# A fused sparse attention and gated FFN on one core: PV turned round for the strided heads, exp kept in PSUM, masks of the first batch by TensorE, stores by SyncE

## The chip, the cores and the metric

The kernel runs on one core of a Trainium2 chip. Times are device microseconds; a time is the median of several executions. The profile has its own measure, the span from the first to the last instruction of one profiled execution.

TensorE is the matrix engine (PE in the profile, PEld its weight loads), DVE the vector engine, ACT the scalar engine, POOL GpSimd, SP or SyncE the engine that issues loads. SBUF and PSUM are the two memories in which the program places its tiles; in both kernels every matmul writes a PSUM tile (`ps_...` and `mps` in the views). PV is the product of the masked probabilities with V, U the transposes that turn its result back. A filler is a matmul whose result nobody uses, put where the planner saw TensorE wait in the start. Distances between the starts of matmuls are read from the single records of the trace, which the views shown here merge.

## The reference, cut to what matters

```python
# q, k, v: (8 batches, 8 heads, 576 positions, 64)
scores = q @ k.T / 8
# heads 0-3: causal band of 32;  heads 4-7: causal, key % 32 == query % 32
attn = softmax(where(mask, scores, -1e9)) @ v
x = attn -> (4608 tokens, 512)
out = ((x @ w1) * (x @ w2)) @ w3 @ w_out       # widths 1024, 1024, 512
```

The kernel multiplies `w3 @ w_out` once at its start (W34 below), so that the FFN is two products (a, b), one elementwise product, and one product with W34 (o).

## The kernel before

Heads are handled in pairs; pairs 0 and 1 are local, pairs 2 and 3 strided. Positions are grouped so that a local block has 96 queries and a strided block 72, with at most 128 keys each. Every pair is done in two halves g. A planner inside the program sorts all operations of all engines into fixed orders by a list of costs; so the order of each engine is static, and an engine that waits holds back everything behind it (TensorE for 1.60 us in the hole shown below). Attention of batch b+1 is woven into the FFN of batch b.

The parts that the change touches, shortened:

```python
# scores, keys on partitions: PSUM slot "B" (two of them); then exp to SBUF, then mask in SBUF
matmul(sps[:, h, i*w:(i+1)*w], kT[r_, ks:ks+P], qT[r_, hp, qs:qs+w])
pte = att.tile([P, 2, 288], FP16)
scalar.activation(out=pte, in_=sps, func=Exp, scale=scale)      # ACT; frees the slot
vector.tensor_mul(ptm, pte, mask)                               # DVE, both inputs in SBUF
# PV, old form: weights = ptm (128 columns, zero padded), streamed = [V | 1]  (65 columns)
matmul(xps[:, h, i*65:(i+1)*65], ptms[pslot][0:kr, c0:c0+P], vt[0:kr, ..., :])
# out: queries on partitions; column 64 is the sum.  Normalise, transpose back (U), copy to xT
vector.reciprocal(rcp, xv[..., D]);  vector.tensor_mul(xqs, xv[..., 0:D], rcp)
tensor.transpose(ps_U[:, t*w:(t+1)*w], xqs[...], id16);  copy(xT[hp][:, S*b:S*b+S], ps_U)
# ... FFN tiles a, b, mul, o ...; the stores are issued by ACT
```

The softmax here doesn't subtract the row's maximum and nothing guards it: scores larger than these inputs give would overflow.

## Time and profile before

| | before |
|---|---|
| time, median of 3 runs | 281.95 us (281.72 to 282.17) |
| the profiled execution | 283.71 us, span 282.0 us |
| TensorE busy | 96% |
| first FFN matmul | 42.3 us |
| first FFN matmul to the start of the last matmul | 235.9 us |

Busy times of the engines, granted TensorE clock in 40 slices, and shares of the chain that ended last, from the page of the kernel before:

```profile
PE 270.5 (96%) x2540; PEld 150.5 (53%) x2540; DVE 166.3 (59%) x326; ACT 155.4 (55%) x291; POOL 123.2 (44%) x146
...
PEclk9999999999999999999999999999999999999999
...
PE 83%; DMA 8%; DVE 4%; SPq 1%; ACT 1%; POOL 1%; issue 0%; ACTq 0%; POOLq 0%; DVEq 0%
```

TensorE is nearly always busy (96%), at full clock (mean granted 1.000). The next lines are the engine table over stretches of the span of the kernel before. Its columns are the stretch, its length, then busy time and instruction count of PE, PEld, DVE, ACT and POOL, then clock, DMA share and GB/s.

```profile
30.00:40.00 10.00, 9.95 (x145) 8.62 (x142) 6.21 (x15) 6.04 (x13) 9.58 (x12) 1.00 1.04 339
40.00:50.00 10.00, 9.11 (x108) 5.87 (x107) 6.67 (x14) 6.85 (x15) 8.99 (x10) 1.00 1.09 354
...
120.00:140.00 20.00, 18.39 (x169) 9.65 (x166) 13.64 (x23) 11.32 (x21) 12.70 (x15) 1.00 0.86 267
140.00:160.00 20.00, 20.00 (x213) 11.25 (x213) 13.89 (x26) 12.61 (x24) 10.63 (x13) 1.00 0.65 185
```

From 60 us on TensorE is full in nearly every stretch (19.82 of 20 at 80 to 100), with one hole at 120 to 140 us (18.39 of 20). From 30 to 50 us the DMA engines are full (share 1.04 and 1.09) and POOL, which casts everything that is loaded to fp16, has 9 of 10 us. A busy TensorE is not yet one that runs at its peak, so I also read the distance from one matmul's start to the next: 216 ns for a 512-column FFN matmul, 56 for a 128-column transpose, 30 for PV.

The hole is in the timeline (start, duration, engine, line, what, and in brackets the idle time before it with what ended it):

```profile
132.74 4.07 DVE L669 TENSOR_TENSOR ptm<-pte,maskL 128x576 f16<-128x576 f16 x2
...
133.27 1.04 POOL L290 CAST v16S<-st 96x1024 f16<-96x1024 f32 x1
...
134.25 2.25 POOL L290 CAST x<-st 128x1024 f16<-128x1024 f32 x2
135.66 0.35 PE L682 MATMUL ps_X<-v16L,ptm 128*128 128x65 f16 x6 [1.60 <-DVE ptm L669]
```

Two mask products on DVE took 4.07 us together while POOL ran casts without a break, and TensorE waited 1.60 us in front of the PV that needed one of them. The groups by shape (busy us, mean ns of one, then idle time) show the same products, and the TensorE parts that the change touches:

```profile
L669 DVE TENSOR_TENSOR ptm<-pte,maskS 96x576 f16<-96x576 f16 x32 | 22.0, 726 | 0.2 <-ACT pte L661 0.2
...
L708 PE MATMUL ps_U<-id,xqs 72*128 72x72 f16 x128 | 6.9, 199 | 0.0
...
L682 PE MATMUL ps_X<-v16L,ptm 128*128 128x65 f16 x192 | 10.8, 194 | 1.6 <-DVE ptm L669 1.6
...
L682 PEld LDWEIGHTS <-ptm 128*128 128x128 f16 x192 | 9.7, 98 | 7.8 <-DVE ptm L669 2.1
```

A mask product has a mean of 726 ns, but after 180 us, where POOL has nothing more to do, each takes 445. The first FFN matmul of the kernel before stands here:

```profile
41.93 0.43 PE L650 MATMUL ps_S<-qT,kTS 64*128 64x72 f16 x16 [0.70 <-ACT kTS L286]
42.30 1.04 PE L740 MATMUL ps_a<-xT,w1h 128*128 128x512 f16 x4
```

### The profile page before, as it was taken

What the parts mean: (1) busy time and instruction counts of PE and PEld (TensorE: products, weight loads), DVE (VectorE), ACT (ScalarE), POOL (GpSimd) and SP (SyncE); (2) the same over time, 40 slices, a digit from 0 to 9 for tenths busy, and PEclk for the clock granted to TensorE, in tenths of its full rate; (3) what the DMA queues carried; (4) which work ended last, traced back from release to release, by engine and by line L of the source; (5) the groups of instructions that cost most, each with busy time, mean ns of one, the idle gap of its engine ahead of it and who ended that gap; (6) DMA issues with size and microseconds to landing.
All of it is one profiled execution on the core that took longest, in us unless ns stands there. A gap on an engine that the chain in (4) does not pass through costs nothing.

```text
span 282.0 us, 6430 instructions
## 1 busy us (share of the span) xinstructions
PE 270.5 (96%) x2540; PEld 150.5 (53%) x2540; DVE 166.3 (59%) x326; ACT 155.4 (55%) x291; POOL 123.2 (44%) x146
## 2 busy tenths in 40 slices
PE   4989989999999999999799999999999999999995
PEld 1468876456555555555455555555555554444443
DVE  4037486876668788856885668466746673320320
ACT  2386576448665665666357656765666543324322
POOL 5876898699669685772956352100000000000000
PEclk9999999999999999999999999999999999999999
DMA  6999999996779678978973800210021003003003
GB/s 222 323 376 358 279 357 355 240 294 235 246 185 356 170 241 243 278 248 233 337 159 102 302 2 2 94 58 0 3 112 40 0 4 147 2 0 149 0 3 149
DMA packets 53679, 48.66 MB, mean 173 GB/s; under 512 B 21008, under 2 KB 45840, under 8 KB 53648
## 3 DMA queue, kind: packets, MB, share of 16 engines
q1 hardware_dynamic: 48320, 38.81, 46.2%
q10 hardware_dynamic: 5328, 9.44, 8.9%
q8 instruction: 20, 0.33, 0.5%
q14 instruction: 11, 0.09, 0.1%
HBM read 38.80 MB, written 9.44 MB: 171 GB/s over the span
## 4 chain that ended last, share of the span: by engine, by line
PE 83%; DMA 8%; DVE 4%; SPq 1%; ACT 1%; POOL 1%; issue 0%; ACTq 0%; POOLq 0%; DVEq 0%
PE ps_a L740 22%; PE ps_b L757 21%; PE ps_o L777 21%; PE ps_X L682 5%; PE ps_T L614 4%; DMA st<-in_moe_w_dram 4%; PE ps_S L650 4%; PE ps_U L708 3%; DMA st<-in_moe_w_out_dram 3%; DVE ptm L669 3%; PE ps_mm L543 3%; DMA st<-in_k_dram 2%; SPq L293 1%; DVE xT L288 1%; DVE abt L763 0%; ACT qT L286 0%
## 5 line engine op out<-in xcount | busy, mean ns | idle before, releaser
L763 DVE TENSOR_TENSOR abt<-ps_b,asb 128x512 f16<-128x512 f32 x72 | 49.5, 688 | 53.8 <-PE ps_b L757 53.2
L740 PE MATMUL ps_a<-xT,w1h 128*128 128x512 f16 x288 | 74.0, 379 | 0.0
L757 PE MATMUL ps_b<-xT,w2h 128*128 128x512 f16 x288 | 73.9, 379 | 0.0
L286 ACT COPY asb<-ps_a 128x512 f32<-128x512 f32 x72 | 42.5, 590 | 48.0 <-PE ps_a L740 48.0
L777 PE MATMUL ps_o<-w,abt 128*128 128x512 f16 (+1 forms) x296 | 67.3, 373 | 0.0
L661 ACT ACTIVATE pte<-ps_S 96x576 f16<-96x576 f32 (+1 forms) x64 | 38.4, 648 | 12.4 <-PE ps_S L650 12.3
L757 PEld LDWEIGHTS <-w2h 128*128 128x128 f16 x288 | 27.3, 98 | 30.7
L777 PEld LDWEIGHTS <-abt 128*128 128x128 f16 x296 | 27.2, 98 | 27.0
L697 DVE TENSOR_TENSOR xqs<-ps_X,rcp 72x512 f16<-72x512 f32 (+1 forms) x64 | 39.7, 620 | 2.2
L290 POOL CAST x<-st 128x1024 f16<-128x1024 f32 x32 | 34.7, 1102 | 11.5 <-DMA st<-in_k_dram 4.1
L740 PEld LDWEIGHTS <-w1h 128*128 128x128 f16 x288 | 25.7, 98 | 23.9
L286 ACT COPY osb<-ps_o 128x512 f32<-128x512 f32 (+1 forms) x37 | 21.9, 591 | 27.3 <-PE ps_o L777 27.3
L290 POOL CAST v16L<-st 32x768 f16<-32x768 f32 (+1 forms) x32 | 27.6, 864 | 14.0 <-DMA st<-in_v_dram 4.7
L286 ACT COPY qT<-ps_T 128x512 f16<-128x512 f16 x27 | 15.8, 586 | 28.1 <-PE ps_T L614 28.0
L682 PEld LDWEIGHTS <-ptm 96*128 96x128 f16 (+1 forms) x448 | 21.4, 97 | 15.3 <-DVE ptm L669 3.5
L288 DVE COPY xT<-ps_U 128x576 f16<-128x576 f16 x30 | 17.9, 596 | 12.2 <-PE ps_U L708 12.2
L696 DVE RECIPROCAL rcp<-ps_X 72x8 f32<-72x8 f32 (+1 forms) x64 | 12.4, 193 | 17.8 <-PE ps_X L682 17.0
L290 POOL CAST v16S<-st 96x1024 f16<-96x1024 f32 x16 | 16.8, 1054 | 13.4 <-PE ps_X L682 12.4
L669 DVE TENSOR_TENSOR ptm<-pte,maskL 128x576 f16<-128x576 f16 x32 | 21.8, 713 | 0.8 <-ACT pte L661 0.7
L669 DVE TENSOR_TENSOR ptm<-pte,maskS 96x576 f16<-96x576 f16 x32 | 22.0, 726 | 0.2 <-ACT pte L661 0.2
L614 PE MATMUL ps_T<-id,x 128*128 128x128 f16 x256 | 19.1, 219 | 0.0
L543 PE MATMUL ps_mm<-woh,w3T 128*128 128x256 f16 x128 | 16.5, 273 | 0.7 <-ACT w3T L286 0.7
(65 smaller groups left out, 235.8 us busy)
## 6 DMA issues: line engine op xcount, KB each, us to landing
out_dram<-osb ACTq DMA_DIRECT2D x35, 256.0 KB, 2.0
st<-in_q_dram SPq DMA_DIRECT2D x16, 512.0 KB, 4.4
st<-in_k_dram SPq DMA_DIRECT2D x16, 512.0 KB, 7.4
st<-in_moe_w_dram SPq DMA_DIRECT2D x16, 512.0 KB, 7.9
st<-in_v_dram SPq DMA_DIRECT2D x32, 144.0 KB, 5.3
st<-in_v_dram SPq DMA_DIRECT2D x16, 256.0 KB, 5.0
st<-in_moe_w_out_dram SPq DMA_DIRECT2D x4, 512.0 KB, 7.5
st<-in_q_dram SPq DMA_DIRECT2D x8, 128.0 KB, 5.3
```

The costliest lines, as they stand in the source:

```text
L286: pin(nc.scalar.copy(out=out, in_=in_))
L290: pin(nc.gpsimd.tensor_copy(out=out, in_=in_))
L543: pin(nc.tensor.matmul(ps, big[f"w3T{kc // 4}"][:, kc % 4, js], big["woh"][:, kc, ns], start=(kc == 0), stop=(kc == KF - 1)))
L614: pin(nc.tensor.transpose(ps[:, c * P:(c + 1) * P], x16[(b, x, hp // 2)][:, c, h0:h0 + 2] .rearrange("p h d -> p (h d)"), id16))
L661: pin(nc.scalar.activation(out=pte[0:kr], in_=bank("B", sk)[0:kr, :, 0:288], func=AF.Exp, bias=0.0, scale=scale))
L669: pin(nc.vector.tensor_mul(ptm[0:kr, 0:576].rearrange("p (a x) -> p a x", x=w), pte[0:kr].rearrange("p h (a x) -> p (h a) x", x=w), _ap(mk ...
L682: pin(nc.tensor.matmul(xps[:, h, i * 65:(i + 1) * 65], ptms[pslot][0:kr, c0:c0 + P], vt[0:kr, 2 * (hp % 2) + h, g * m + i, :], start=True, ...
L697: pin(nc.vector.tensor_mul(xqs[0:w, 0:m].rearrange("p i h d -> p h i d"), xv[:, :, :, 0:D], _ap(rcp, 0, [[rcp.ap[0][0], w], [4, 2], [1, m] ...
L740: pin(nc.tensor.matmul(ps, w1h[:, ci, js], xT[ci][:, tok], start=(ci == 0), stop=(ci == KM - 1)))
L757: pin(nc.tensor.matmul(ps, w2h[:, ci, js], xT[ci][:, tok], start=(ci == 0), stop=(ci == KM - 1)))
L763: pin(nc.vector.tensor_mul(big[("abt", t)][:, jc, :], bank("f", f"b{t}_{jc}"), live[("asb", t, jc)]))
L777: pin(nc.tensor.matmul(ps, big[("abt", t)][:, ci, bass.ds(ts * P, P)], w34[:, ci, bass.ds(pt * nw, nw)], start=(ci == 0), stop=(ci == KF - ...
```

## The change

Its intent: in the old PV form the result has queries on partitions and must be transposed back. If `[V | ones]` becomes the weights and the masked probabilities are streamed, the result already has the head dimension on partitions, and 64 columns of ones put the sum on 64 more partitions. The reciprocal of the sum is then exp(-ln(sum)) on ACT; exp and ln come from one table set here (the changed kernel's profile has a single table load, of 1.28 us). This is done for the strided pairs from batch 1 on. The diff, cut to its core:

```diff
+    pin(nc.scalar.preload_act_table_set("natural_log_exp_and_others"))
-    NSTG = 9                                   # staging buffers of loads
+    NSTG = cfg.get("nstg", 8)                  # set to 7
-    v16S = [... [KB, 4, ST, D + 1] ...]; ptms = [... [P, 640] ...]    # padded with zeros
+    v16S = [... [KB, 4, ST, P] ...];     ptms = [... [P, 576] ...]
+    nc.vector.memset(v16L[0][:, :, :, D:P], 1.0); nc.vector.memset(v16S[0][:, :, :, D:P], 1.0)
 # scores of both halves in one group; batch 0: mask added before exp (pm)
+    pin(nc.tensor.matmul(sps[:, h, 0:m * w], id16[0:kr], bias, start=True, stop=False))
 # exp in place in PSUM, mask product reads PSUM
-    pin(nc.scalar.activation(out=pte[0:kr], in_=bank("B", sk)..., func=AF.Exp, ...))
+    pin(nc.scalar.activation(out=sps, in_=sps, func=AF.Exp, bias=0.0, scale=scale))
 # PV, old form (local pairs, batch 0): only w weight columns
-    ptms[pslot][0:kr, c0:c0 + P]
+    ptms[pslot][0:kr, c0:c0 + w]
 # PV, new form (strided pairs from batch 1 on)
+    pin(nc.tensor.matmul(xps[:, h, i * w:(i + 1) * w], vt[0:kr, 2 * (hp % 2) + h, g * m + i, :],
+                         ptms[pslot][0:kr, h * 288 + i * w:h * 288 + (i + 1) * w], ...))
+    pin(nc.scalar.activation(out=xps, in_=xps, func=AF.Ln, ...))            # partitions 64 to 127
+    pin(nc.scalar.activation(out=rcp, in_=i, func=AF.Exp, scale=-1.0))
+    pin(nc.vector.tensor_mul(o, i0, i1))                                    # straight into xT
 # stores
-    {"SP": 450} if t >= cfg.get("stsp", 99) else {"ACT": 345}
+    cfg.get("st", {"SP": 450})
 # start: other order of loads; batch 0's attention ranks behind the first W3 transposes
-    base = {0: -60, 1: 95}
+    base = {0: 40, 1: 60}
```

Smaller edits (cut): one DMA instead of two for a local V, a loop order in two evictions, the planner's costs.

## The prediction

> **What bounds it now.** TensorE. The page gives it 96% busy and, by the engine table over windows, 20.0 of every 20 us from 60 us on, except 80 to 100 (19.8) and 120 to 140 (18.4). From start-to-start distances in the trace: FFN matmuls 216 ns each (about 187 us in all), transposes 56, scores pairs about 40, PV 30, strided U transposes 37 to 39. The span splits at the first FFN matmul (42.4 us in the timeline). Before it the start is bound by loads and casts (DMA share 1.0 or more from 5 to 55 us, POOL 4.4 to 4.9 of 5 us from 30 to 50); TensorE has 24 us of work there plus 34 filler matmuls and waits. After it come 231 us of work at those distances, about 4.5 us of small waits (the longest 1.8 us at 133.7, where PV waits for DVE's mask product) and a 3.8 us tail.
>
> **TensorE work changed.**
> - 112 strided U transposes go: -4.5 us.
> - The new strided PV streams 72 columns for 65: 30 to about 32.5 ns, x224: +0.6 us.
> - Local PV (192) and batch 0's strided PV now load 96 and 72 weight columns; the padding to 128 is gone. [...] At the trace's start 128 columns loaded in 103 ns, 96 in 155. [...] I estimate about 42 ns per PV for 30: +2.3 us.
> - 16 mask matmuls of 288 columns: about +2 us, in the start, where TensorE partly waits anyway.
> After the first FFN matmul about 230 us remain: only 1 us less.
>
> **Other engines.** The mask product (fp16, both inputs in SBUF) took 445 ns after 180 us, where POOL has ended, but 800 to 820 on average before and up to 2.87 us. [...] Reading PSUM it should take a steady 750 ns (128x512 FFN products take 690), and waits such as the one at 133.7 should vanish. Batch 0's eight products go. DVE loses 28 reciprocals, 28 norm products of 687 ns and 14 copies of xT, gains 56 products of about 455 ns: 166 to about 180 us busy. ACT gains 56 logs and exps of 0.65 us: 155 to about 195, but loses 37 store issues of 338 ns, not counted as busy. Both keep slack. Chains lengthen (scores, exp, mask, PV, ln, exp, product hold the same two PSUM slots), so new small waits of TensorE before scores are likely.
>
> **Start.** Nearly the same loads precede the first FFN weights; 24 fillers instead of 34. I expect the first FFN matmul at 41 us (39 to 43).
>
> **Sum.** 41 + 230.3 + 3.5 of waits + 3.8 = 278.5 us; range 275.5 to 282.5. Chances: faster by over 2% 0.17, within 0.78, slower 0.05.
>
> **What would show it.** Mask products steady near 750 ns with no TensorE wait of over 1 us after 60 us; local PV at about 42 ns; the first FFN matmul at 39 to 43 us; one table load; stores on SyncE with no new DMA starvation.
>
> **What would make it wrong.** Weight loads of 96 columns that do not hide at all (80 ns per PV: +7 us); the two PSUM slots held too long, so that TensorE waits at each scores group (+5 us or more); a better fed start, which would take it below 276.

## The result, and the profile after

| | before | after |
|---|---|---|
| time, median | 282.06 us (281.72 to 282.33, 4 runs) | 280.87 us (280.58 to 281.00, 4 runs) |
| ratio | | 0.9957 (95%: 0.994 to 0.9974) |
| span of the profiled execution | 282.0 us | 279.1 us |
| first FFN matmul | 42.3 us | 43.0 us |
| from there to the last matmul's start | 235.9 us | 232.5 us |
| last matmul's start to the end | 3.8 us | 3.5 us |

The kernel is 0.4% faster: inside the range, but 1.1 to 1.2 us where a gain of 3.5 was forecast.

The same parts of the page of the changed kernel:

```profile
PE 267.4 (96%) x2434; PEld 151.3 (54%) x2434; DVE 173.9 (62%) x328; ACT 173.9 (62%) x321; POOL 118.0 (42%) x146
...
PE 95%; DVE 4%; issue 0%; ACT 0%; DVEq 0%
```

DMA has gone from the chain that ended last: it is 95% TensorE. The engine table over the same stretches of the changed kernel:

```profile
30.00:40.00 10.00, 10.00 (x146) 8.76 (x145) 5.99 (x15) 6.32 (x14) 9.75 (x12) 1.00 1.08 356
40.00:50.00 10.00, 10.00 (x106) 6.26 (x103) 7.58 (x14) 7.75 (x17) 7.68 (x9) 1.00 1.08 359
...
120.00:140.00 20.00, 20.00 (x194) 11.07 (x192) 13.74 (x27) 13.54 (x27) 9.28 (x12) 1.00 0.61 197
140.00:160.00 20.00, 20.00 (x193) 10.87 (x190) 14.22 (x28) 15.64 (x30) 6.79 (x8) 1.00 0.52 168
```

The hole is gone; in the full table TensorE has no free time from 30 us until the last stretch, which holds the tail. The groups by shape of the changed kernel:

```profile
L774 ACT ACTIVATE rcp<-ps_X 64x576 f32<-64x576 f32 x28 | 18.1, 647 | 0.9
L763 ACT ACTIVATE ps_X<-ps_X 64x576 f32<-64x576 f32 x28 | 17.7, 631 | 0.9 <-PE ps_X L724 0.5
...
L712 DVE TENSOR_TENSOR ptm<-ps_S,maskS 96x576 f16<-96x576 f32 x28 | 19.9, 749 | 1.3 <-ACT ps_S L704 0.5
...
L734 PE MATMUL ps_X<-v16L,ptm 128*96 128x65 f16 x192 | 13.1, 207 | 0.0
L734 PEld LDWEIGHTS <-ptm 128*96 128x96 f16 x192 | 12.8, 124 | 4.2
L724 PE MATMUL ps_X<-ptm,v16S 96*128 96x72 f16 x224 | 11.9, 196 | 0.0
```

Mask products take a steady 749 ns. A local PV has 207 ns for 194, and its weight load of 96 columns takes 124 ns for the 98 of 128 columns. Starts of successive local PVs are 45 ns apart in the median (42 on average within a group), where they were 30. The start of the changed kernel:

```profile
2.41 1.34 DVE L382 MEMSET v16L<- 128x1536 f16 x1 [0.27 <-issue]
4.13 1.76 DVE L384 MEMSET v16S<- 96x2048 f16 x1 [0.38 <-issue]
...
6.98 0.22 DVE L373 TENSOR_TENSOR maskK<-mps,causal 72x72 f16<-72x72 f32 x1
7.26 0.22 PE L371 MATMUL mps<-maskK,place 72*96 72x72 f16 x1 [4.18 <-DVE maskK L373]
7.29 4.08 PE L328 MATMUL ps_spin<-w 128*128 128x512 f16 x9
```

The two fills of ones delay the mask building on DVE and so TensorE's second matmul: it starts at 7.26 us, and TensorE waits 4.18 us for it. (In the kernel before it started at 4.09.) TensorE then goes through nine filler matmuls, most of them 427 ns apart where later ones are 216, and its first useful work, a W3 transpose, starts at 11.16 us. The first FFN matmul:

```profile
39.29 1.04 POOL L308 CAST w1h<-st 128x1024 f16<-128x1024 f32 x1
...
42.66 0.43 PE L686 MATMUL ps_S<-qT,kTS 64*128 64x72 f16 x16
...
43.02 1.04 PE L838 MATMUL ps_a<-xT,w1h 128*128 128x512 f16 x4
```

Its weights were being cast at 39.29 us, 1.2 us earlier than in the kernel before (40.51), but TensorE still had work ahead of it in its order.

### The profile page after: what moved, and what is told of

Its sections match the earlier page's. It is cut to its first block, busy times and chain, and to the rows that moved or that the text cites. A ratio compares the mean times of both kernels' runs of the same rounds, so it can differ in the third digit from the quotient of the medians.

```text
span 279.1 us, 6299 instructions
## 1 busy us (share of the span) xinstructions
PE 267.4 (96%) x2434; PEld 151.3 (54%) x2434; DVE 173.9 (62%) x328; ACT 173.9 (62%) x321; POOL 118.0 (42%) x146
## 4 chain that ended last, share of the span: by engine, by line
PE 95%; DVE 4%; issue 0%; ACT 0%; DVEq 0%
PE ps_o L874 23%; PE ps_b L854 22%; PE ps_a L838 22%; PE ps_T L643 5%; PE ps_mm L571 5%; PE ps_S L686 4%; PE ps_X L734 3%; PE ps_X L724 3%; PE ps_spin L328 2%; PE ps_U L803 2%; PE ps_tr L552 1%; DVE v16S L384 1%; PE ps_R L596 1%; PE ps_S L677 1%; DVE xqs L753 0%; DVE v16L L382 0%
## 5 line engine op out<-in xcount | busy, mean ns | idle before, releaser
L304 ACT COPY asb<-ps_a 128x512 f32<-128x512 f32 x72 | 42.2, 589 | 40.2 <-PE ps_a L838 39.4
L704 ACT ACTIVATE ps_S<-ps_S 96x576 f32<-96x576 f32 (+1 forms) x56 | 32.9, 628 | 11.0 <-PE ps_S L686 10.5
L304 ACT COPY osb<-ps_o 128x512 f32<-128x512 f32 x35 | 20.6, 588 | 18.5 <-PE ps_o L874 18.2
L790 DVE TENSOR_TENSOR xT<-ps_X,rcp 64x288 f16<-64x288 f32 x56 | 25.1, 448 | 5.6 <-ACT rcp L774 5.0
L712 DVE TENSOR_TENSOR ptm<-ps_S,maskL 128x576 f16<-128x576 f32 x28 | 19.8, 750 | 12.0 <-ACT ps_S L704 12.0
L753 DVE TENSOR_TENSOR xqs<-ps_X,rcq 96x384 f16<-96x384 f32 (+1 forms) x36 | 20.5, 568 | 1.2
L712 DVE TENSOR_TENSOR ptm<-ps_S,maskS 96x576 f16<-96x576 f32 x28 | 19.9, 749 | 1.3 <-ACT ps_S L704 0.5
L774 ACT ACTIVATE rcp<-ps_X 64x576 f32<-64x576 f32 x28 | 18.1, 647 | 0.9
L763 ACT ACTIVATE ps_X<-ps_X 64x576 f32<-64x576 f32 x28 | 17.7, 631 | 0.9 <-PE ps_X L724 0.5
L306 DVE COPY qT<-ps_T 128x512 f16<-128x512 f16 x16 | 11.1, 692 | 9.6 <-PE ps_T L643 8.3
L734 PEld LDWEIGHTS <-ptm 128*96 128x96 f16 (+1 forms) x224 | 14.2, 123 | 4.3
(80 smaller groups left out, 278.1 us busy)
```

Of the source, the lines that this page charges most:

```text
L304: pin(nc.scalar.copy(out=out, in_=in_))
L704: pin(nc.scalar.activation(out=sps, in_=sps, func=AF.Exp, bias=0.0, scale=scale))
L712: pin(nc.vector.tensor_mul(ptm[0:kr, 0:576].rearrange("p (h a x) -> p h a x", h=2, x=w), pte[0:kr].rearrange("p h (a x) -> p h a x", x=w), ...
L734: pin(nc.tensor.matmul(xps[0:w, h, i * 65:(i + 1) * 65], ptms[pslot][0:kr, c0:c0 + w], vt[0:kr, 2 * (hp % 2) + h, g * m + i, 0:D + 1], sta ...
L753: pin(nc.vector.tensor_mul(xqs[0:w, 0:m].rearrange("p i h d -> p h i d"), xv[:, :, :, 0:D], _ap(rcp, 0, [[rcp.ap[0][0], w], [4, 2], [1, m] ...
L790: pin(nc.vector.tensor_mul(o, i0, i1))
```

## The experiments

Kernels of one call share a chip and the runs of the kernel before. "Stretch" is the time from the first FFN matmul to the last matmul's start, read from the profiled execution. It repeats closely (232.54, 232.55, 232.54, 232.54 and 232.55 in five traces that share the changed kernel's order after the start), while the first FFN matmul moves by more than 1 us between executions of one kernel (42.3 and 43.3 for the kernel before).

| run | time (us) | before | ratio to before | first FFN matmul | stretch |
|---|---|---|---|---|---|
| b_again | 283.46 | 283.33 | 0.9989 | 43.3 | 233.55 |
| e_pad | 278.13 | 283.33 | 0.9812 | 42.3 | 230.43 |
| e_memset | 280.16 | 283.33 | 0.9881 | 43.1 | 232.55 |
| e_pad_memset | 277.05 | 283.33 | 0.9792 | 41.5 | 230.44 |
| a_again | 281.19 | 282.79 | 0.9927 | 43.2 | 232.54 |
| e_sbexp | 282.84 | 282.79 | 0.9986 | 42.0 | 234.64 |
| e_oldpv | 285.15 | 282.79 | 1.0073 | 42.2 | 236.59 |
| e_local_pad | 299.63 (3 fast runs; 301.10 of all 6) | 282.79 | 1.0549 | 42.0 | 252.41 |
| e_pad2 | 278.32 | 283.12 | 0.9846 | 42.5 | 230.44 |
| e_nopm_pad | 278.36 | 283.12 | 0.9843 | 42.1 | 230.97 |
| e_stact_pad | 278.85 | 283.12 | 0.9856 | 43.0 | 230.43 |
| e_oldload_pad | 279.79 | 283.12 | 0.9896 | 45.5 | 228.81 |
| a_again2 | 280.64 | 283.19 | 0.9916 | 43.1 | 232.54 |
| e_memset2 | 279.70 | 283.19 | 0.9897 | 42.0 | 232.55 |
| e_pad_memset2 | 277.41 | 283.19 | 0.9797 | 42.1 | 230.43 |
| e_oldload_padmem | 279.73 | 283.19 | 0.9882 | 45.0 | 228.81 |

All gave correct results.

### Was the first profile of the kernel before a typical one?

The kernel before, unchanged.

> The kernel before, unchanged, profiled again. Theory 1 (the prediction was anchored on an untypical profile): the profiled execution of before took 283.71 us where its median was 281.95, so this trace will have a span near 280.3 us (time minus span 1.7 us as in the changed kernel) and will lack most of the 1.77 us TensorE wait at 133.7 us. Rival (the wait is part of the fixed schedule and the time has another offset): span near 282 again, with that wait again, at a time near 282.

The profiled execution had a time of 282.38 us and a span of 280.6, and TensorE's wait for a mask product at that place was 0.2 us instead of 1.77 (from start to start; the profile's idle time there was 1.60). The local PV group of this trace has no idle time, where the first profile had 1.6 us:

```profile
L682 PE MATMUL ps_X<-v16L,ptm 128*128 128x65 f16 x192 | 10.8, 194 | 0.0
```

So that wait is not part of every execution, and the first profile was of an execution 1.76 us above its median. Mask products still stretch here, up to 2.84 us, but none held up TensorE for long. On this chip the median itself was 283.46. Why is not shown: only the execution of 282.38 us was traced, and its first FFN matmul came at 43.3 us, 1.0 later than in the first profile, while its stretch was 2.36 us shorter. The kernel before scatters: 281.95 to 285.29 us in eleven runs of one call, where the changed kernel had 280.08 to 281.44 in the next.

### The narrow weights

```diff
-    ptms = [consts.tile([P, 576], FP16, ...) for i in range(4)]
+    ptms = [consts.tile([P, 640], FP16, ...) for i in range(4)]      # last 64 columns zero
-    matmul(xps[0:w, h, i * 65:(i + 1) * 65], ptms[pslot][0:kr, c0:c0 + w], ...)
+    matmul(xps[:, h, i * 65:(i + 1) * 65], ptms[pslot][0:kr, c0:c0 + P], ...)
```

> The changed kernel with the zero padding of the masked weights and 128 weight columns for the old-form PV restored (192 local and 32 batch-0 products). Theory: narrow weight loads cost 45 ns per local PV for 30, so this is 2.0 to 2.6 us faster than the changed kernel (about 278.5 us), with PV back at 30 ns. Rival: the load width is hidden or other waits take its place: under 0.5 us.

> The changed kernel with the padding, again, as the partner of the next three on this chip: about 278.1 us, stretch after the first FFN matmul 230.4 us, 3.0 us (1.1%) below the changed kernel by the ratios to before.

Groups by shape of the padded kernel, second run:

```profile
L736 PE MATMUL ps_X<-v16L,ptm 128*128 128x65 f16 x192 | 10.7, 193 | 0.0
L736 PEld LDWEIGHTS <-ptm 128*128 128x128 f16 x192 | 9.5, 97 | 4.8
```

The load is back at 97 ns and starts of local PVs are 30 ns apart. The stretch is 2.1 us shorter, nearly all of it in the local PV of that stretch (7.11 to 5.07 us, by distances between starts). The products in the start give another 0.4 us. The time is 278.1 to 278.3 us. The padding is worth 2.3 us (277.41 for 279.70) and 3.1 us (277.05 for 280.16), both with the fills moved. The theory holds in these times: the change had dropped the padding to 128 columns, and loading fewer columns made each load longer, 97 ns for 128 columns and 124 for 96. The runs do not show why.

### Exp in SBUF again, in the same order

The order of every engine stays as it is; only where exp writes and what the mask product reads is changed.

```diff
-    activation(out=sps, in_=sps, func=AF.Exp, ...)             # PSUM, in place
-    tensor_mul(ptm, sps, mask)
+    activation(out=ptms[pslot], in_=sps, func=AF.Exp, ...)     # SBUF
+    tensor_mul(ptm, ptm, mask)                                 # both inputs in SBUF
```

> The changed kernel with the same order on every engine, but exp writes its fp16 result to SBUF and the mask product works on that in place, so both its inputs are in SBUF as before the change. Theory: while POOL runs (to about 175 us) mask products stretch from 750 ns to 800 on average with some over 2 us, POOL casts lengthen by 60 ns, and TensorE gets back waits of 0.3 to 2 us, so 0.3 to 3 us slower and with more scatter. Rival: the waits at 133 us in the first profile were chance and cost nothing in the median: within 0.3 us; the masks fall to 445 ns after 180 us.

One place of the timeline in this run:

```profile
71.18 3.25 DVE L712 TENSOR_TENSOR ptm<-ptm,maskL 128x576 f16<-128x576 f16 x2 [0.46 <-ACT ptm L701]
...
71.87 2.24 POOL L308 CAST v16S<-st 96x1024 f16<-96x1024 f32 x2
...
74.48 0.46 PE L734 MATMUL ps_X<-v16L,ptm 128*96 128x65 f16 x6 [0.87 <-DVE ptm L712]
```

The same place in the changed kernel:

```profile
71.88 2.02 POOL L308 CAST v16S<-st 96x1024 f16<-96x1024 f32 x2
72.23 1.42 DVE L712 TENSOR_TENSOR ptm<-ps_S,maskL 128x576 f16<-128x576 f32 x2 [0.45 <-ACT ps_S L704]
...
74.44 0.42 PE L734 MATMUL ps_X<-v16L,ptm 128*96 128x65 f16 x6
```

With both inputs in SBUF, two mask products beside two POOL casts take 3.25 us, the casts 2.24, and TensorE waits 0.87 us in front of its PV. From PSUM they take 1.42 and 2.02, and PV starts without a wait. After 180 us the products fall to 455 ns. So the PSUM form is 300 ns slower when POOL is quiet, and worth it because POOL is busy until shortly before 180 us. The median is 1.65 us higher than the changed kernel's and the traced stretch 2.1 us longer. But the time scatters from 280.49 to 284.36, and the intervals of the two ratios overlap (0.9935 to 1.0036 and 0.9894 to 0.996), so the size is rough. Why products and casts take longer there is not shown, only these times.

### The old PV form for all pairs

```diff
-    nx=4,
+    nx=32,      # strided pairs of all batches: old PV, U transposes, no ln and exp of sums
```

> The changed kernel with the old PV form for all pairs (transposes U back, no ln and exp of sums), order replanned. It loads 72 weight columns in strided PV. Theory from distances: U back +3.7 us, strided PV 35 ns for 32.5 +0.6: 4 us slower, stretch after the first FFN matmul near 236.7 us. Rival: the new form's longer chains cost waits that hide this gain: under 2 us slower.

The planner made a new order for this run. The time is 4.0 us higher (285.15 for 281.19), the stretch 4.05 us longer: U +3.73 us, strided PV +0.46. The rest is small. No wait of the new form ate its gain. The old form here loads 72 columns, unpadded: its strided PV takes 7.73 us, 6.80 in the kernel before with padding. So 0.9 of the 4.0 us is again the dropped padding; against a padded old form I estimate a gain of about 3.3 us. The ratio to the kernel before, 1.0073, says something else: without the turned PV, what remains of the change is a loss.

### The new PV form for the local pairs too

```diff
-    new=(2, 3)
+    new=(0, 1, 2, 3)
```

with the padding for batch 0.

> The changed kernel with the new PV form for local pairs too (96 columns streamed, 128 weight columns), and with the padding back for batch 0. Theory from distances: against e_pad U goes (-3.8 us) and local PV grows from 30 to 41 ns (+1.8): stretch after the first FFN matmul 228.5 us, time about 276 us. Rival: ACT (up by some 36 us of ln and exp) and the held PSUM slots make TensorE wait: 278 or more.

The rival was right, and far beyond its number: 296.25 to 300.05 us in three fast runs. (Three more, of 302.14 to 306.47 us, count as slow; their mean granted clocks were 0.960 to 0.972, those of the fast three 0.976 to 0.987.) TensorE now waits in front of the scores for DVE's last product of the pair before, as the two PSUM slots are held until then. One such place in the timeline, and the engine table around it:

```profile
159.83 0.30 PE L688 MATMUL ps_S<-qT,kTL 64*128 64x96 f16 x6 [1.25 <-DVE xT L792]
160.78 0.42 PE L688 MATMUL ps_S<-qT,kTL 64*128 64x96 f16 x6 [0.64 <-DVE xT L792]
161.14 1.89 PE L840 MATMUL ps_a<-xT,w1h 128*128 128x512 f16 x4
```

```profile
157.00:159.00 2.00, 1.59 (x26) 1.24 (x24) 0.82 (x2) 1.94 (x4) 1.24 (x2) 1.00 0.86 251
159.00:161.00 2.00, 0.52 (x12) 0.43 (x12) 1.57 (x4) 1.96 (x4) 1.76 (x2) 0.93 0.68 248
161.00:164.00 3.00, 3.00 (x13) 1.03 (x8) 1.42 (x2) 2.27 (x4) 0.00 (x0) 0.50 0.14 57
164.00:167.00 3.00, 3.00 (x24) 1.61 (x23) 0.85 (x2) 1.55 (x3) 0.72 (x1) 0.98 0.10 36
```

After the two waits (1.25 and 0.64 us) the granted clock is 0.50 for three microseconds, and the FFN matmuls start about 427 ns apart (four from 161.14 to 162.82 us) where they were 216. So the waits are paid, and then part of the speed. From the 0.93, 0.50 and 0.98 of the last three rows I estimate the time at 0.50 as 3.4 us. The page's clock line, in slices of 7.45 us, falls to 0.7, 0.8, 0.8 and 0.7 in the slices that start at 156, 186, 223 and 253 us. Not each such pair of waits did it: in the slices around 70, 100 and 130 us TensorE's busy share falls to 0.7 as well, and the clock stays at 0.9 or more. What separates the two cases is not shown.

### Masks of batch 0, stores, order of loads

On top of the padded kernel, each part of the change undone alone (the planner made a new order for each):

```diff
-    pm=4,                                     # e_nopm_pad
+    pm=0,
-    cfg.get("st", {"SP": 450})                # e_stact_pad
+    {"ACT": 345}
-    base = {0: 40, 1: 60}; new order of loads # e_oldload_pad
+    base = {0: -60, 1: 95}; old order
```

> The padded kernel with batch 0's masks multiplied on DVE as before, not added on TensorE (16 matmuls, 3.2 us of TensorE's start, go; eight DVE products of 0.75 us come). Theory (the start is bound by loads and casts): TensorE only waits or spins longer, first FFN matmul where it was within 1 us, time within 0.7 us of the padded kernel. Rival (the start is bound by TensorE): 2 to 3 us faster.

> The padded kernel with stores issued by ACT as before (37 issues of 0.34 us on its queue). Theory: ACT has slack, so within 0.5 us. Rival: issues delay ACT's exp, ln and evictions and TensorE waits: 1 to 3 us slower.

> The padded kernel with the load order and start ranks of the kernel before (attention of batch 0 first, not the W3 transposes). Theory (the new start gained nothing, as the first FFN matmul is at 42 to 43 us in both): within 0.7 us. Rival: the old order is 1.5 to 3 us slower, and the new start was a real part of the gain.

The masks on TensorE change nothing: 278.36 for 278.32. Their 3.2 us in TensorE's start go, and TensorE's fillers and waits grow instead (fillers 9.3 us for 7.8). This fits a start that is bound by loads and casts. Stores by ACT have a median 0.5 us higher, but the runs overlap (278.18 to 279.39, and 277.96 to 279.41), so this is not shown in the time. The stretch is the same (230.43), so ACT's issues delay nothing in it; the trace has 0.5 us more at the end (4.01 us after the last matmul's start for 3.53), and the first FFN matmul was also 0.5 us later in that execution. The old load order costs 1.5 us (279.79 for 278.32), so the rival is right here: the new start is a part of the gain. It does not show against the kernel before, because the new kernel with the old order has its first FFN matmul at 45.5 us, where the kernel before had it at 42.3 to 43.3. (More of the W34 work stands before it in that order, so its stretch is 1.6 us shorter, and the net is 1.5.)

### The late fills

```diff
-    nc.vector.memset(v16S[0][:, :, :, D:P], 1.0)          # scheduled before the masks
+    pin(nc.vector.memset(v16S[0][:, :, :, D:P], 1.0))     # program order: after the masks
```

and likewise for the local V and for the four mask instructions in front.

> The changed kernel with the two long fills of ones on DVE (1.34 and 1.76 us) put after the building of the masks. Theory: the mask matmul, and so all of TensorE's fixed order, starts 3 us late behind those fills, and TensorE's backlog carries that to the first FFN matmul (43.0 us where its weights were cast at 40.3): first FFN matmul at 40.3 to 41, 2 to 2.7 us faster. Rival: the start is bound by loads and casts: under 0.7 us.

> Both of these edits. If they are independent: 4 to 5 us faster than the changed kernel, about 276.3 us; if the start is bound by loads, about 278.5.

> The changed kernel, unchanged, as the partner on this chip. TensorE's stretch from the first FFN matmul to its last start should repeat to 0.1 us (232.5 us; 232.54 and 232.55 in two traces), while the first FFN matmul moves with loads between 41.5 and 43.5 us.

> The changed kernel, unchanged, as the partner on this chip: about 281 us, first FFN matmul at 43 us.

> The changed kernel with the fills of ones after the masks, again. Theory (the start is bound by loads and casts, the head start is waited away): median within 0.7 us of the changed kernel of this call, with larger scatter. Rival (TensorE's late start binds): 2 us or more faster.

> Padding and moved fills, again: 3 to 4 us below the changed kernel of this call; stretch after the first FFN matmul 230.4 us.

> The padded kernel with the old load order and start ranks and with the fills moved. If the late fills are what puts the first FFN matmul at 45.5 us with the old order: back to 43 us, 2 us faster than with the fills early (279.8). If it is the fewer staging buffers (7 for 9) and replanned order: within 0.7 us of 279.8.

TensorE's work in the start, with the fills moved (second run):

```profile
3.46 0.22 PE L371 MATMUL mps<-maskK,place 72*96 72x72 f16 x1 [0.39 <-DVE maskK L373]
...
7.36 1.06 PE L552 MATMUL ps_tr<-id,w3n 128*128 128x128 f16 x8
...
26.34 0.61 PE L552 MATMUL ps_tr<-id,w3n 128*128 128x128 f16 x8
28.30 0.62 PE L552 MATMUL ps_tr<-id,w3n 128*128 128x128 f16 x8 [1.34 <-POOL w3n L308]
...
41.96 1.04 PE L838 MATMUL ps_a<-xT,w1h 128*128 128x512 f16 x4
```

The mask matmul now starts at 3.46 us and the first W3 transposes at 7.36, 3.8 us earlier than in a_again2 (11.12). But at 27 us TensorE waits 1.34 us for the cast of the next block of W3, and the first FFN matmul is at 42.0 us, 1.1 us earlier than in a_again2 (43.1). The medians differ by 0.94 us (279.70 for 280.64). So neither side of the expectation was right. Most of the head start is waited away on loads and casts, and about 1 us remains (0.6 by the means, as one of the six runs took 281.88). In e_memset's trace even that did not show (43.1). Padding and moved fills together took 277.05 us and padding alone 278.13; e_pad_memset had expected 276.3 if the two are independent and 278.5 if loads bind, and lies between. With the old order of loads the fills change nothing (279.73, where 279.79 was measured, ratios 0.9882 and 0.9896): what makes that order slow in the new kernel is not the fills. The seven staging buffers (nine before) and the replanned order remain as suspects. Nine do not fit beside the new tiles, nor do eight (the build refuses both), so this stays open.

With padding and moved fills the kernel takes 277.05 and 277.41 us, ratios 0.9792 (0.975 to 0.9834) and 0.9797 (0.9775 to 0.982) to the kernel before: it beats both kernels.

## Why the prediction was right or wrong

**The direction and the class were right, the size was wrong.** Forecast was -3.5 us; -1.1 to -1.2 us was measured (-1.6 and -2.55 us between the medians of two later calls, in which the kernel before was slower).

**The step that failed: the sum.** "41 + 230.3 + 3.5 of waits + 3.8 = 278.5 us" (the terms give 278.6) adds up parts of a span, and I wrote the result down as a time. The time is 1.7 us more. I missed it because in the kernel before the span of the profile (282.0) happened to equal the median time (281.95): the profiled execution was 1.76 us slower than the median, and the two cancelled. The wait of 1.77 us that b_again does not have is about as long. The sum against the measured span, term by term:

| term | predicted | measured |
|---|---|---|
| first FFN matmul | 41 | 43.0 |
| work and waits after it | 233.8 | 232.5 |
| tail | 3.8 | 3.5 |
| span | 278.6 (written 278.5) | 279.1 |
| span to time | 0 | 1.7 |
| time | 278.5 | 280.8 (median 280.87) |

This also shows which gains did not come. The -3.5 us were about 1.3 in the start (42.3 to 41), 1 of work and 1 of waits. Measured against b_again, an execution near the first call's median (282.38 for 282.06), the stretch fell by only 1.0 us (233.55 to 232.54), about the work alone: b_again has hardly any of the waits that the forecast removes. Its start is 0.3 us later than the changed kernel's (43.3 for 43.0).

**The second step: the start, mis-sized by 2 us.** I counted fillers (24 for 34) and took their number for a head start. The order listing does not show when TensorE can begin: the fills of ones put its second matmul at 7.26 us. Moving them away brought 1 us, not the 2 us missing, and e_nopm_pad shows that work taken off TensorE here is worth nothing: the start is mostly bound by loads and casts, and the first FFN matmul moves by over 1 us from execution to execution even in one kernel.

**What was right.** Narrow weight loads: predicted 42 ns per local PV, measured 45 in the median and 42 on average, cost predicted 2.3 us, measured 2.1 in the stretch and 0.4 in the start. The nearness is partly luck: the forecast was an estimate from one load of 128 columns of 103 ns and one of 96 columns of 155, but most loads of 128 columns in that start took 147 ns, and with those the same estimate gives far less. U and the strided PV, from the kernel before to the changed one: -3.7 and +0.46 us for the -4.5 and +0.6 predicted (37 to 39 ns were read for a strided U, the trace has 33); e_oldpv gives 4.0 in time. Mask products at 750 ns, and no TensorE wait of over 1 us after 60 us. One table load. That longer chains would cost new waits was wrong for the strided pairs (e_oldpv) and right for the local ones (e_local_pad). ACT was predicted at 195 us busy and has 173.9: I missed that the planner moved copies to DVE (about 15 us of ACT's busy time), and that the evictions of the rest rows kept ACT busy for 7.7 us instead of 14.0. (The order of the loops changed in half of the 32, but the durations of the others fell too, kTS from 811 to 472 ns; this was not tested alone, so the cause is open.) In both profiles ACT has at most 1% of the chain that ended last.

**Where the expected gain went.** Measured one at a time, the turned PV is worth 4.0 us (0.9 of it dropped padding), exp in PSUM roughly 1.65, the new start 1.5, the stores 0.5 that the scatter does not confirm, the masks nothing. That is some 7 us if they add up, which no run tests. Against it stand 2.3 to 3.1 us for the dropped padding, as measured, and a start that came no sooner. That second part is seen (45.5 us with the old order in the new kernel), but its cause in the change is not settled.

## What to carry to other kernels

Try the stationary operand of small matmuls at 128 columns, padded with zeros: here 128 columns loaded in 97 ns and 96 in 124, local PVs started 30 and 45 ns apart, and dropping unused columns cost two thirds of what removing 112 transposes gained. Where a DVE product of two SBUF inputs runs beside POOL casts, an input in PSUM can be slower by itself and still better, since it takes the scatter away (749 ns throughout, for 445 ns to 2.87 us). Before a forecast in a few microseconds, find out how far the profiled execution lies from the median, and what lies between its span and the time.
